# Score blocks trimmed of their masked corner in 64x64 tiles, and another written-out order of the later steps, in a fused window-attention and swish kernel

## The chip, the cores and the metric

The kernel runs on one core of a Trainium2 chip. The core has a matrix engine (PE in the profile, its weight loads PEld), three engines for elementwise work (DVE, ACT, POOL), and DMA queues (those of SP, POOL and ACT are used here). The metric is the device time of one execution in microseconds. Three executions of the kernel before took 222.1, 220.78 and 221.57 us; their median, 221.57 us, is the time before.

## What is computed

Attention with a sink of 4 keys and a window of 128 keys, over 4 batches, 8 heads, 768 positions and 64 features per head; the result goes, as 3072 tokens of 512 features, through a two-layer network with a swish that has a factor beta per hidden feature:

```python
pos = np.arange(S)                                  # S = 768
rel = pos[:, None] - pos[None, :]
keep = (pos[None, :] < n_sink) | ((rel >= 0) & (rel < window))   # n_sink 4, window 128
scores = np.where(keep, q @ k.T / sqrt(64), -1e9)   # per batch and head
attn = softmax(scores) @ v
x = attn as [3072 tokens, 512]
h = x @ w_in                                        # [512, 2048]
g = h * (1 / (1 + exp(-beta * h)))
out = g @ w_out                                     # [2048, 512]
```

A query block of 128 positions therefore needs its own key block (kept where the key does not lie after the query), the key block before it (kept where the key lies less than 128 back, which is the opposite triangle), and the four sink keys.

## The kernel before

**Units and tiles.** Two heads of one half of a batch (384 positions, three blocks of 128) make a unit; there are 32, four to each of eight half batches. Half batches 0, 2, 4, 6 hold key and query blocks 0 to 2 of a batch (called even below), half batches 1, 3, 5, 7 blocks 3 to 5 (odd). Blocks of scores, 128 keys by 128 queries, are of three kinds: `s` (key block 0 with its sinks), `d` (a query block with its own key block, the diagonal) and `p` (a query block with the key block before it: the "next" block, seen from the key). Four blocks of one kind of place make a tile, which lies in two PSUM banks, one for each head, and becomes one buffer `E` after the exponential (L887, ACT, 1024 columns) and two masks (POOL L902, or DVE L896 and L906). `tiles_of` lists the tiles. In the odd half batches from number 3 on, a pair of units has three tiles: `dpdp` for each unit (key blocks 3 and 4, each with two query blocks side by side) and one tile of four lone blocks, `ddpp`: own block 5 of both units and next block 2 to 3 of both. Even half batches have a tile `dddd` of lone own blocks.

**Steps.** Work for the matrix engine is cut into steps, written as letters in the string `later` and executed in its order, except that a planner (`Graph.arrange`) may take one of the next three groups first when it expects the first one to wait. T: transposes of q and k (L726). S: a burst of up to three score tiles (`SC`, and `band` for half batches 2 and up, L825), its exponentials and masks, and in some the sink scores of a half batch (L918). A: the product with v of one unit (L963, L974), or of four units at once for units 20 to 23 and 28 to 31 (L947, L974), and the division by the sum of weights (DVE L978, L980). R: the transposition of the result; from unit 12 on it is a transposing DMA on SP's queue and has no matrix work. H: 128 hidden features for 384 tokens, four matmuls of 384 columns (L1018), the tanh (ACT L1023) and the product (DVE L1025). O: four of the sixteen matmuls of 512 columns of an output block of 128 tokens (L1041); the fourth such step of a block ends with the eviction (ACT L524 or DVE L530) and the store, which is issued from POOL's queue (L1059).

H0 is the first H step, and so on. H(16T+m) makes hidden block m of token group T (384 tokens). O steps from O12 on: O(12T+4t+j) is part j of block t of group T, needs the hidden blocks 4j to 4j+3 of the group, and keeps one PSUM bank from part 0 to part 3. A8 is the unit 8; the letters that take four units at once are called A20 and A28 here. S8 to S20 go through `band`; S11, S12, S15, S16, S19 and S20 are the six bursts of odd half batches, and each holds two tiles `dpdp` and one `ddpp`. S8 holds the two tiles of units 8 and 9, S9 the tile `dddd` of half batch 2 and one tile of units 10 and 11, S10 the last tile of these units.

**Score matmuls of `band`.** The array is used as four sub-arrays of 64 rows by 64 columns: the row half is the head (64 features of contraction), the column half `c` the half of the key block (64 keys). For a key block with both its own and its next query block (`dp`), each half `c` streams 192 of the 256 queries, from 64c on, since the rest is masked for these keys. All other key blocks stream all their columns: 256 for `s`, 128 for a lone `d` or `p`:

```python
a, z_ = (KW * c, 128 + KW * c + KW) if kinds == "dp" else (0, 128 * len(cols))   # KW = 64
```

The four matmuls of a key block (c = 0, 1, and the two heads for each) follow one another, then those of the next key block. In `band` the numbers 3.5 ns and `(z_ - a) / 2.4 + 2` are only the planner's estimates.

**Queues.** Each engine runs its own list in order. The planner deals out casts, masks and evictions among ACT, DVE and POOL, and lays down the order of SP's and POOL's DMA issues, with estimated costs.

Of the kernel before, what the change touches and what calls it, by code (L numbers as in the profile page):

```python
# [395 lines left out]
def _program(nc, G, sb, ps, q, k, v, w_in, w_out, beta, out):  # L396
    NU = 2 * NPAIR
    NSTG, NX, NV, NT, NE, NON, NG, NTT, NOS, NWS = 2, 2, 3, 12, 7, 6, 3, 3, 4, 6
# [4 lines left out]
    NK = NB // 2  # L403
# [17 lines left out]
    qkT = sb("qkT", (128, NT, 2, HALF), BF16)  # L421
# [24 lines left out]
    BAND, KW = 8, 64  # L446
    LANES, QUADS = [6,7], [5,7]
    P = ps("P", (128, 8, 512))

    def add(eng, fn, ns, r=(), w=(), x=(), dma=None, after=(), hold=550, chain=None):  # L450
        return G.add(eng, fn, ns, r, w, x, dma, None, after, hold, chain)
# [237 lines left out]
    def qk_keys(u, name="qkT", every=NT):  # L689
        return [(name, u % every, a, c) for a in range(2) for c in range(NK)]  # L690
# [111 lines left out]

    def band(tiles, bs):

        got, free, now = [], {}, 0.0
        for j, t_ in enumerate(tiles):
            jobs = {}
            for i, (kind, u, kb, qb) in enumerate(TILES[t_]):
                jobs.setdefault((u, kb), []).append((qb, i, kind))
            for (u, kb), cols in sorted(jobs.items(), key=lambda x: x[1][0][1]):  # L810
                half = u // 4 % 2
                own_ = u if kb >= NK * half else u - 4
                kc, q0, i0 = (kb % NK) * 128, (cols[0][0] - NK * half) * 128, cols[0][1]
                kinds = "".join(x[2] for x in cols)
                for c in range(2):
                    a, z_ = (KW * c, 128 + KW * c + KW) if kinds == "dp" else (0, 128 * len(cols))
                    for hh in range(2):
                        rows = slice(64 * hh, 64 * hh + 64)
                        at = max(now, free.get((hh, c), 0.0))
                        if got:  # L820
                            got[-1][3] = at - now
                        now, free[hh, c] = at + 3.5, at + (z_ - a) / 2.4 + 2
                        got.append([lambda e, rows=rows, own_=own_, kc=kc, u=u, q0=q0, a=a, z_=z_, bk=bs[2 * j + hh],
                                    i0=i0, c=c:
                                    e.matmul(P[KW * c:KW * c + KW, bk, 128 * i0 + a:128 * i0 + z_],  # L825
                                             qkT[rows, own_ % NT, 1, kc + KW * c:kc + KW * c + KW],
                                             qkT[rows, u % NT, 0, q0 + a:q0 + z_], start=True, stop=True),
                                    qk_keys(u) + (qk_keys(own_) if own_ != u else []), bs[2 * j + hh], 0.0])
        got[-1][3] = max(free.values()) - now
        for fn, keys, bk, ns in got:  # L830
            add("pe", fn, ns + 3.5, r=keys, x=[("B", bk)])

    def SC(n):
# [18 lines left out]
        if TILES[tiles[0]][0][1] >= BAND:  # L852
            band(tiles, bs)
# [382 lines left out]
    for x in "T0:63 T1:01 S1:01 T2:64 T3:46 S0:12 S4:56 S3:34 S2:01 F:2 V:5 A1:1 A0:5 A2:4 R0:5 A3:2 R1:0 R2:4 R3:0".split():  # L1236
        x, _, bk = x.partition(":")
# [5 lines left out]
        elif x == "F":  # L1243
            G.begin()
            bk = take(1)
# [9 lines left out]
    for x in "".split():  # L1255
        x, _, bk = x.partition(":")
# [20 lines left out]
    for x in early:  # L1277
# [5 lines left out]
        if x[0] == "T":  # L1283
# [3 lines left out]
                OT=4 + sum(x[0] == "R" for x in early), H=sum(x[0] == "H" for x in early), load=24)  # L1287
    n_cast[0], n_w[0] = 20, 8
    last = "O"
    later = ("AAAAHOORORORROHHHHHHHHHHTTOTOOSTOOOOSSOOHHHAAAAHHRHRRORHOOOSOOOOOSAROARHHHHARHARHHHHHHHHHH"  # L1290
             "OOOOOOSOOOOSOOHHHARARARARHHHHHHHHHHHHHOOOOOOSOOOOOSOHHHHHHHHHHHHHHHHARRRROOOOSOOOSOOOOARAR"
             "ARARHHHHHHHHHHHHHHHHHHHHHHHHHOOOSOOOOOSOOOHHHHHARRRRHHOOOOOOOOHHHHHHHHHHHHHHHHOOOOOOOOOOOO"
             "OOOOOOOOOO")
    for c in later:
        s = {"S": "SC", "R": "OT", "A": "AV"}.get(c, c)
        while True:
# [4 lines left out]
            now = G.free["pe"]  # L1301
# [41 lines left out]
```

## Time and profile before

| | us |
|---|---|
| median of three executions | 221.57 (220.78 to 222.10) |
| the profiled execution, its own time | 222.19 |
| its span, first to last instruction | 220.1 |
| lies around the span | 2.1 |

The profiled execution is 0.62 us above the median. The span is divided below into what the matrix engine does and what it waits for; a group's row gives the busy time, the mean length of one instruction in ns (which overlaps its neighbours', because matmuls are pipelined), and the idle time before it with what ended it. The chain of waits gives start, length and the work or wait, with the number of instructions.

### The profile page before, as it was taken

The numbers are of one execution on the slowest core, as the hardware profiler recorded it, in microseconds if no ns is written. First come the engines' busy times: TensorE is split into PE (matmuls) and PEld (weight loads), VectorE is DVE, ScalarE is ACT, GpSimd is POOL, SyncE is SP. The second block draws the span as 40 slices with busy tenths as digits, with TensorE's granted clock in tenths as the row PEclk, the third lists the DMA queues.
The fourth block names the chain that finished last, engine by engine and source line by source line (L and its number), as shares of the span: only waits on it lengthen the run. The fifth ranks groups of instructions, "written<-read, shape, count | busy, mean of one in ns | idle before, by whom it ended". The sixth has DMA issues, their size and how long they took to land.

```text
span 220.1 us, 4804 instructions
## 1 busy us (share of the span) xinstructions
PE 211.7 (96%) x1893; PEld 120.2 (55%) x1915; DVE 136.1 (62%) x297; ACT 148.8 (68%) x245; POOL 69.2 (31%) x132
## 2 busy tenths in 40 slices
PE   8889899999999999999999999999999999999995
PEld 2455457565475466546654566546665456465443
DVE  2687699898786379444980489557885248088000
ACT  2698799586875897459774698195987674187211
POOL 8213552211550682036202761152101770100100
PEclk9999999999999999999999999999999999999999
DMA  6999989999979999599975999879859022400122
GB/s 195 234 292 362 354 212 370 387 316 211 209 168 149 223 172 258 81 220 218 216 120 135 209 209 202 170 167 246 119 98 189 28 81 53 130 2 0 51 95 95
DMA packets 94718, 39.88 MB, mean 181 GB/s; under 512 B 82072, under 2 KB 89512, under 8 KB 94696
## 3 DMA queue, kind: packets, MB, share of 16 engines
q1 hardware_dynamic: 91928, 33.28, 70.6%
q0 software_dynamic: 1680, 5.51, 7.6%
q10 hardware_dynamic: 1088, 0.79, 1.1%
q8 instruction: 15, 0.25, 0.5%
q14 instruction: 7, 0.06, 0.1%
HBM read 27.37 MB, written 6.29 MB: 153 GB/s over the span
## 4 chain that ended last, share of the span: by engine, by line
PE 83%; SPq 7%; DMA 5%; DVE 3%; issue 1%; ACT 0%
PE P L1041 37%; PE P L1018 35%; DMA g<-in_moe_w_in_dram 5%; PE P L974 4%; SPq L605 4%; PE P L825 4%; SPq L617 2%; DVE E L906 1%; PE P L963 1%; SPq L1252 1%; DVE g L1025 1%; PE P L726 1%; DVE w_in L529 1%; PE P L1000 1%; PE P L918 1%
## 5 line engine op out<-in xcount | busy, mean ns | idle before, releaser
L1018 PE MATMUL P<-xT,w_in 128*128 128x384 bf16 x512 | 87.0, 326 | 1.3 <-POOL w_in L526 1.0
L1041 PE MATMUL P<-w_out,g 128*128 128x512 bf16 (+2 forms) x380 | 83.5, 370 | 1.7 <-issue 1.0
L1023 ACT ACTIVATE t<-P,hbeta 128x384 f32<-128x384 f32 x128 | 71.8, 586 | 17.9 <-PE P L1018 13.2
L1025 DVE SCALAR_TENSOR_TENSOR g<-t,P 128x384 bf16<-128x384 f32 x128 | 67.7, 551 | 20.8 <-ACT t L1023 15.9
L1018 PEld LDWEIGHTS P<-xT,w_in 128*128 128x128 bf16 x512 | 49.0, 98 | 34.3 <-POOL w_in L526 1.4
L1041 PEld LDWEIGHTS P<-w_out,g 128*128 128x128 bf16 x400 | 37.3, 98 | 40.4 <-issue 0.5
L887 ACT ACTIVATE E<-P 128x1024 bf16<-128x1024 f32 x44 | 43.2, 1032 | 11.4 <-PE P L825 10.9
L902 POOL TENSOR_SCALAR_AFFINE_SELECT E<-E 128x512 bf16<-128x512 bf16 x57 | 36.8, 670 | 31.8 <-ACT E L887 31.7
L1059 POOL DMA_DIRECT2D out_dram<-osb x21 | 11.9, 568 | 57.9 <-ACT osb L524 57.9
L524 ACT ACTIVATE osb<-P 128x512 f32<-128x512 f32 x13 | 7.8, 598 | 25.5 <-PE P L1041 25.5
L980 DVE TENSOR_TENSOR onorm<-P,rden 128x384 bf16<-128x384 f32 x32 | 17.8, 555 | 0.9
L974 PE MATMUL P<-vaug,E 128*128 128x65 bf16 x352 | 15.1, 193 | 0.0
L530 DVE TENSOR_SCALAR osb<-P 128x512 f32<-128x512 f32 x10 | 6.9, 690 | 13.0 <-PE P L1041 12.9
L974 PEld LDWEIGHTS P<-vaug,E 128*128 128x128 bf16 x352 | 14.1, 97 | 1.3
L529 DVE CAST vaug<-v_stage 128x512 bf16<-128x512 f32 x19 | 9.5, 502 | 8.4 <-DMA v_stage<-in_v_dram 8.3
L896 DVE TENSOR_TENSOR E<-E,maskS 128x512 bf16<-128x512 bf16 x16 | 7.0, 464 | 8.6 <-ACT E L887 8.5
L1261 PE MATMUL P<-const-bfloat16-1.0 128*128 128x512 bf16 (+1 forms) x35 | 11.2, 443 | 1.1 <-PEq L1325 0.8
L524 ACT ACTIVATE k<-k_stage 128x512 bf16<-128x512 f32 (+1 forms) x13 | 7.8, 603 | 2.1 <-DMA k_stage<-in_k_dram 2.0
L825 PEld LDWEIGHTS P<-qkT 64*64 64x64 bf16 x336 | 6.4, 106 | 5.2 <-issue 4.7
L698 POOL TENSOR_TENSOR kS<-qkT,headm 128x8 bf16<-128x8 bf16 (+1 forms) x10 | 2.3, 230 | 22.1 <-DMA qkT<-k 12.7
L825 PE MATMUL P<-qkT 64*64 64x192 bf16 (+2 forms) x336 | 8.7, 239 | 0.0
L526 POOL TENSOR_SCALAR_AFFINE_SELECT q<-q_stage 128x512 bf16<-128x512 f32 x6 | 4.1, 690 | 14.2 <-DMA q_stage<-in_q_dram 14.2
(66 smaller groups left out, 123.2 us busy)
## 6 DMA issues: line engine op xcount, KB each, us to landing
v_stage<-in_v_dram SPq DMA_DIRECT2D x24, 256.0 KB, 4.7
out_dram<-osb POOLq DMA_DIRECT2D x21, 256.0 KB, 3.0
q_stage<-in_q_dram SPq DMA_DIRECT2D x15, 256.0 KB, 5.2
k_stage<-in_k_dram SPq DMA_DIRECT2D x15, 256.0 KB, 5.2
wst<-in_moe_w_in_dram SPq DMA_DIRECT2D x5, 512.0 KB, 8.2
wst<-in_moe_w_out_dram SPq DMA_DIRECT2D x4, 512.0 KB, 7.6
g<-in_moe_w_out_dram SPq DMA_DIRECT2D x4, 512.0 KB, 6.6
q_stage<-in_q_dram SPq DMA_DIRECT2D x2, 768.0 KB, 7.8
```

The source lines that it names most:

```text
L524: return lambda e: e.activation(dst, src, AF.Copy, bias=0.0, scale=scale)
L529: return lambda e: e.tensor_copy(dst, src)
L825: e.matmul(P[KW * c:KW * c + KW, bk, 128 * i0 + a:128 * i0 + z_], qkT[rows, own_ % NT, 1, kc + KW * c:kc + KW * c + KW], qkT[rows, u % NT, ...
L887: add("act", lambda e, src=src, dst_=dst_: e.activation(dst_, src, AF.Exp, bias=0.0, scale=SCALE), act_ns(1024), w=[("E", z)] + [("m", z, ...
L902: alts = {"gp": (lambda e, dd=dd, sg=sg: e.affine_select(dd, dd, [[0, n] for n in dd.shape[1:-1]] + [[sg, 128]], ALU.is_ge, 0.0, base=min( ...
L974: e.matmul(A[:, c0:c0 + D + 1], E[t_ % NE][:, i, hh, :], vaug[vz][:, kb % NK, 2 * hp + hh, :], start=a, stop=o, skip_group_check=True), 31,
L980: add("dve", lambda e: e.tensor_tensor(onorm[on][:, :, :, :].rearrange("p m h d -> p (m h) d"), av[:, :, 0:D], rden[on][:, :].unsqueeze(2) ...
L1018: add("pe", lambda e, c=c: e.matmul(hp, w_in16[:, c, m * 128:(m + 1) * 128], xT[:, c, t0:t0 + HALF], start=(c == 0), stop=(c == 3)), mm_ns ...
L1023: add("act", lambda e: e.activation(tt[ti][:, :], hp, AF.Tanh, bias=0.0, scale=hbeta[:, m:m + 1]), act_ns(HALF) + 93, r=["hbeta"], w=[("t" ...
L1025: add("dve", lambda e: e.scalar_tensor_tensor(gt[T_ % NG][:, m, :], tt[ti][:, :], 1.0, hp, ALU.add, ALU.mult), dve_ns(HALF), r=[("t", ti)] ...
L1041: add("pe", lambda e, m=m: e.matmul(P[:, bk, 0:n], gt[T_ % NG][:, m, t * 128:(t + 1) * 128], w_out16[:, m, cols], start=(m == 0), stop=(m ...
L1059: add(eng, lambda e: e.dma_start(out_t[3 * T_ + t], osb[z][:, :]), 262144 / 300, r=[("osb", z)], dma=f"do{eng}{z}", hold={"sp": 550, "gp": ...
```

## The change

Two things are changed. First, in `band`, a lone own block (`d`) streams for the keys 64 to 127 only the queries 64 to 127, and a lone next block (`p`) streams for the keys 0 to 63 only the queries 0 to 63; the corners left out are masked to zero later in any case, by a select that overwrites them. In tiles of four lone blocks the blocks are issued in the order 0, 2, 1, 3 (own, next, own, next in a `ddpp`), and a `p` issues its long half first. The planner's estimate for a score matmul is half a ns longer. Second, thirteen steps of the string `later` change place; the kinds of steps and their number are the same. Read by their numbers, the moves are these:

| step | before | after |
|---|---|---|
| H28 | ahead of A8 | behind A9 |
| H33 | behind R13 | ahead of O23 |
| O24 | behind H47 | ahead of H45 |
| H51 | behind R19 | ahead of A16 |
| R19 | behind A19 | behind H56 |
| O36 | behind H63 | behind H57 |
| S16 | behind O46 | ahead of O46 |
| O47 | ahead of H64 | behind H67 |
| O52 | behind S17 | ahead of S17 |
| A26 (unit 26) | behind R25 | ahead of R25 |
| O59 | behind H104 | ahead of H104 |
| O69 | ahead of H105 | behind R30 |
| H127 | ahead of O78 | behind O84 |

H28, H33 and so on are counted from H0; an A is named by its unit. All steps before A8 (reached 62 us into the profiled execution) and all behind O84 keep their place, but for what the planner makes of it.

```diff
--- before.py
+++ after.py
@@ -802,30 +802,35 @@
 
     def band(tiles, bs):
 
-        got, free, now = [], {}, 0.0
+        got, free, now, todo = [], {}, 0.0, []
         for j, t_ in enumerate(tiles):
             jobs = {}
             for i, (kind, u, kb, qb) in enumerate(TILES[t_]):
                 jobs.setdefault((u, kb), []).append((qb, i, kind))
-            for (u, kb), cols in sorted(jobs.items(), key=lambda x: x[1][0][1]):
-                half = u // 4 % 2
-                own_ = u if kb >= NK * half else u - 4
-                kc, q0, i0 = (kb % NK) * 128, (cols[0][0] - NK * half) * 128, cols[0][1]
-                kinds = "".join(x[2] for x in cols)
-                for c in range(2):
-                    a, z_ = (KW * c, 128 + KW * c + KW) if kinds == "dp" else (0, 128 * len(cols))
-                    for hh in range(2):
-                        rows = slice(64 * hh, 64 * hh + 64)
-                        at = max(now, free.get((hh, c), 0.0))
-                        if got:
-                            got[-1][3] = at - now
-                        now, free[hh, c] = at + 3.5, at + (z_ - a) / 2.4 + 2
-                        got.append([lambda e, rows=rows, own_=own_, kc=kc, u=u, q0=q0, a=a, z_=z_, bk=bs[2 * j + hh],
-                                    i0=i0, c=c:
-                                    e.matmul(P[KW * c:KW * c + KW, bk, 128 * i0 + a:128 * i0 + z_],
-                                             qkT[rows, own_ % NT, 1, kc + KW * c:kc + KW * c + KW],
-                                             qkT[rows, u % NT, 0, q0 + a:q0 + z_], start=True, stop=True),
-                                    qk_keys(u) + (qk_keys(own_) if own_ != u else []), bs[2 * j + hh], 0.0])
+            mine = []
+            for n, ((u, kb), cols) in enumerate(sorted(jobs.items(), key=lambda x: x[1][0][1])):
+                kind = "".join(x[2] for x in cols)
+                for c in (1, 0) if kind == "p" else (0, 1):
+                    span = {"dp": (KW * c, 128 + KW * c + KW), "d": (KW * c, 128), "p": (0, KW * c + KW)}.get(
+                        kind, (0, 128 * len(cols)))
+                    mine.append((n % 2 if len(jobs) == 4 and kind in "dp" else n, j, u, kb, cols, c, span))
+            todo += sorted(mine, key=lambda x: x[0])
+        for _, j, u, kb, cols, c, (a, z_) in todo:
+            half = u // 4 % 2
+            own_ = u if kb >= NK * half else u - 4
+            kc, q0, i0 = (kb % NK) * 128, (cols[0][0] - NK * half) * 128, cols[0][1]
+            for hh in range(2):
+                rows = slice(64 * hh, 64 * hh + 64)
+                at = max(now, free.get((hh, c), 0.0))
+                if got:
+                    got[-1][3] = at - now
+                now, free[hh, c] = at + 3.5, at + (z_ - a) / 2.4 + 2.5
+                got.append([lambda e, rows=rows, own_=own_, kc=kc, u=u, q0=q0, a=a, z_=z_, bk=bs[2 * j + hh],
+                            i0=i0, c=c:
+                            e.matmul(P[KW * c:KW * c + KW, bk, 128 * i0 + a:128 * i0 + z_],
+                                     qkT[rows, own_ % NT, 1, kc + KW * c:kc + KW * c + KW],
+                                     qkT[rows, u % NT, 0, q0 + a:q0 + z_], start=True, stop=True),
+                            qk_keys(u) + (qk_keys(own_) if own_ != u else []), bs[2 * j + hh], 0.0])
         got[-1][3] = max(free.values()) - now
         for fn, keys, bk, ns in got:
             add("pe", fn, ns + 3.5, r=keys, x=[("B", bk)])
@@ -1287,9 +1292,9 @@
                 OT=4 + sum(x[0] == "R" for x in early), H=sum(x[0] == "H" for x in early), load=24)
     n_cast[0], n_w[0] = 20, 8
     last = "O"
-    later = ("AAAAHOORORORROHHHHHHHHHHTTOTOOSTOOOOSSOOHHHAAAAHHRHRRORHOOOSOOOOOSAROARHHHHARHARHHHHHHHHHH"
-             "OOOOOOSOOOOSOOHHHARARARARHHHHHHHHHHHHHOOOOOOSOOOOOSOHHHHHHHHHHHHHHHHARRRROOOOSOOOSOOOOARAR"
-             "ARARHHHHHHHHHHHHHHHHHHHHHHHHHOOOSOOOOOSOOOHHHHHARRRRHHOOOOOOOOHHHHHHHHHHHHHHHHOOOOOOOOOOOO"
+    later = ("AAAAHOORORORROHHHHHHHHHHTTOTOOSTOOOOSSOOHHAAHAAHHRHRRORHOOOSOOOOOSARHOARHHHARHARHHHHHHHOHH"
+             "HOOOOOSOOOOSOOHHHHARARARAHHHHHRHOHHHHHHOOOOOSOOOOSOHHHHOHHHHHHHHHHHHARRRROOOOOSOOSOOOOARAA"
+             "RRARHHHHHHHHHHHHHHHHHHHHHHHHOHOOSOOOOOSOOHHHHHARRRORHHOOOOOOOOHHHHHHHHHHHHHHHOOOOOOOHOOOOO"
              "OOOOOOOOOO")
     for c in later:
         s = {"S": "SC", "R": "OT", "A": "AV"}.get(c, c)
```

## The prediction

> **What bounds the kernel now.** I read the page's busy times first, then the matrix engine's waits from 32.8 us on, then the chain of waits. 220.1 us of span and 2.1 us around it make the profiled execution's 222.19 us, 0.62 above the median of 221.57. I take differences from the one and add them to the other.
>
> ```profile
> PE 211.7 (96%) x1893; PEld 120.2 (55%) x1915; DVE 136.1 (62%) x297; ACT 148.8 (68%) x245; POOL 69.2 (31%) x132
> ...
> PEclk9999999999999999999999999999999999999999
> ...
> L1041 PE MATMUL P<-w_out,g 128*128 128x512 bf16 (+2 forms) x380 | 83.5, 370 | 1.7 <-issue 1.0
> ...
> L1041 PEld LDWEIGHTS P<-w_out,g 128*128 128x128 bf16 x400 | 37.3, 98 | 40.4 <-issue 0.5
> ```
>
> No other engine comes near PE's 96%, and its granted clock is never under nine tenths. The missing 4% is where a better order would have to earn. The waits of PE over the whole execution:
>
> ```profile
> PE P L1018 <- POOL w_in L526: 1.0, 2, 0.8
> PE P L1041 <- issue: 1.0, 6, 0.2
> ...
> PE P L870 <- DVE qkT L529: 0.8, 1, 0.8
> PE P L1000 <- ACT xT L524: 0.4, 1, 0.4
> ```
>
> Asked from 32.8 us to the last matmul, the same view keeps only the second row, 1.0 us on "issue", in front of O steps. The chain shows what that is:
>
> ```profile
> 105.26 8.45 PE P L1018 x52
> 113.76 5.13 PE P L1041 x23
> 118.89 0.68 PE P L825 x32
> 119.57 0.28 PE P L918 x4
> 119.84 0.16 issue
> 120.00 4.26 PE P L1041 x19
> 124.27 0.68 PE P L825 x32
> 124.95 0.16 issue
> 125.11 0.81 PE P L1041 x3
> ```
>
> O steps have four matmuls each, so x23, x19 and x3 each lack one: the first record behind a wait is missing (380 matmuls against 400 weight loads in L1041). H runs at 8.45/52 = 0.1625 us a matmul. With the missing one, 113.71 (105.26 + 8.45) to 118.89 is 24 matmuls at 0.216 us: no gap between H and O at all. Behind S16, 0.16 + 0.81 = 0.97 us stand for four matmuls, 0.86 us; so about 0.1 us is lost there, at the change from 64x64 sub-arrays to the whole array. After 32.8 us, then, PE waits for nobody; it only pays for changes of array shape. **Moving a step can gain nothing there; it can only uncover something.** Gain must come from fewer or shorter matmuls.
>
> **The tile edit.** The time of a score burst follows its streamed columns. Per sub-array, S14 (two `s` of 256, two `dp` of 192) streams 896 columns, S13 1408 (a `dddd` of 4 x 128 more), an odd burst 4 x 192 + 4 x 128 = 1280 (0.68 us, the rows of S15 and S16 above). S13 and S14:
>
> ```profile
> 95.07 0.73 PE P L825 x32
> ...
> 99.36 0.51 PE P L825 x16
> ```
>
> (0.73 − 0.51)/512 = 0.43 ns and (0.68 − 0.51)/384 = 0.44 ns a column; the rest of the 0.51, some 0.12 us, is the change of shape. In a `ddpp` after the change each sub-array streams 128, 64, 128, 64 columns instead of four times 128: the own block leaves its long half on the lower key half and the next block on the upper, so that in the order own, next, own, next both halves carry 384 columns, not 512. That is 128 x 0.43 = 0.055 us for a burst, and six bursts (S11, S12, S15, S16, S19, S20) give **−0.33 us**. The `dddd` tiles gain nothing: their lower halves still stream four times 128 columns, and the upper halves, now 64, wait for them. Instruction counts stay at 336 in L825; masks and exponentials keep their sizes, and the corner now left unwritten is overwritten by the select.
>
> No row here shows matmuls of two lengths side by side, so bounds: at best −0.33; at worst the two lengths never overlap, each sub-array pair takes (128 + 64) x 4 = 768 columns' time instead of 512, 256 x 0.43 = +0.11 a burst, **+0.66 us** in all. I take −0.33: the rows by shape grow with columns down to the shortest, 32 ns and 30 ns for 64 columns, and halves of `dp` with different columns already run side by side.
>
> ```profile
> L825 PE MATMUL P<-qkT 64*64 64x192 bf16 x144 | 5.2, 247 | 0.0
> ...
> L825 PE MATMUL P<-qkT 64*64 64x128 bf16 x144 | 3.6, 217 | 0.0
> ...
> L825 PE MATMUL P<-qkT 64*64 64x256 bf16 x48 | 2.5, 279 | 0.0
> ```
>
> The Trainium skill speaks against it: "TensorE: Matmul & The Clock Gate", Part 3, "The mechanism", has matmuls start and end strictly in program order. By that rule a 64-column half issued behind a 128-column one could not end before it, a pair would last two long halves, and the term would be 0 instead of −0.33; no run here has two lengths in turn, so nothing shown decides. The same page's LDWEIGHTS section gives columns/1.2 ns, an estimate of 53 ns for 64 columns, which a 64-column matmul would not hide; by that too the term is 0.
>
> **The moves.** The same thirteen steps run elsewhere, so PE's work sums to 0. Changes of shape stay as many: every S still follows an O or stands before one (S16 before O46 instead of O47, S17 behind O52). What remains is cover.
>
> A8 and A9 go ahead of H28. Their last masks, of `dddd`, are the first POOL pair, those of units 10 and 11 the second:
>
> ```profile
> 59.67 1.23 POOL L902 TENSOR_SCALAR_AFFINE_SELECT E<-E 128x512 bf16<-128x512 bf16 x2 [1.34 <-ACT E L887]
> 61.68 1.26 POOL L902 TENSOR_SCALAR_AFFINE_SELECT E<-E 128x512 bf16<-128x512 bf16 x2 [0.77 <-ACT E L887]
> ...
> 60.86 1.95 PE P L1018 x12
> 62.81 0.18 PE P L974 x6
> ...
> 63.53 0.65 PE P L1018 x4
> ```
>
> A8 starts at 62.81 − 0.65 = 62.16 with masks ready at 60.90; A10, behind A8, A9 (0.72) and H28, at 63.53 with masks ready at 62.94. Cover 0.6 us: cost 0; without it at most the 0.65 us that H28 stood for.
>
> O69 behind A28 pulls A28 0.86 us ahead (S20 itself is 0.28 us earlier by then):
>
> ```profile
> 176.38 3.65 POOL L902 TENSOR_SCALAR_AFFINE_SELECT E<-E 128x512 bf16<-128x512 bf16 x6 [0.84 <-ACT E L887]
> ...
> 181.49 0.35 PE L947 MATMUL P<-vS,ES 32*128 32x130 bf16 x12
> ```
>
> It would begin at 180.6; S20's six masks end at 180.03 now. Cover 0.6 us, and more for units 30 and 31, whose masks these are: cost 0, else up to 0.86.
>
> H127 behind O84: O87's last matmul needs its product. From the end of H127's matmuls (202.00) to the end of the last product (203.21) is 1.21 us; O85, O86 and three matmuls of O87 are 11 x 0.216 = 2.4 us. Cost 0.
>
> ```profile
> 191.60 10.40 PE P L1018 x64
> ...
> 200.71 2.50 DVE L1025 SCALAR_TENSOR_TENSOR g<-t,P 128x384 bf16<-128x384 f32 x4
> ```
>
> H51 ahead of A16 gives A16 0.65 us more cover, and H33 the same to A13. O24 and O36 need hidden blocks done by then (H32 to H35; H48 to H51, H51 being moved for it) and hold one of eight banks longer. O47 and O59 carry an eviction on ACT or DVE and a store issued from POOL's queue with them; O47's then fall behind the tanh of H64 to H67 instead of ahead of them, with ACT at 68%, and the masks that the store can delay on POOL are S16's, wanted only by A20 (136.60 in the chain below, S16 at 124.27 above). R19 and the order of R25 and A26 move one transposing DMA on SP's queue each; H64 and H96 need them many microseconds later. O52 ahead of S17 changes nothing: five O steps, O48 to O52, already run between A20 and S17, because the planner had swapped them:
>
> ```profile
> 136.60 1.56 PE P L974 x48
> ...
> 138.21 4.26 PE P L1041 x19
> 142.47 0.73 PE P L825 x32
> ```
>
> Bounds of the moves together: no gain (nothing to gain from), a loss of at most 0.65 + 0.86 = 1.5 us if both thin covers fail. I take 0. What lies before A8 and behind O87 is unchanged. **Sum: −0.33 us**, 222.19 to 221.86 for the profiled execution, 221.57 to 221.24 for the median.
>
> **Rivals.** *No gain in the tiles.* If a short half holds its place until the long one beside it is done, a pair lasts two long halves, a tile four of them as now: 0, 221.57. For it: no row shows two lengths in turn. Against: the halves of `dp`, with different columns, do run side by side. The Trainium skill's "TensorE: Matmul & The Clock Gate" would have it so.
>
> *A mask queued behind a cast: slower.* The changed string moves the planner's clock, and with it which cast POOL gets. POOL takes its list in order and casts wait for loads:
>
> ```profile
> POOL q L526 <- DMA q_stage<-in_q_dram: 14.2, 5, 6.1
> ...
> 102.27 1.23 POOL L902 TENSOR_SCALAR_AFFINE_SELECT E<-E 128x512 bf16<-128x512 bf16 x2 [2.20 <-ACT E L887]
> 103.47 0.66 POOL L526 TENSOR_SCALAR_AFFINE_SELECT q<-q_stage 128x512 bf16<-128x512 f32 x1
> ...
> 103.82 0.18 PE P L974 x6
> ...
> 104.42 0.30 PE P L974 x10
> ```
>
> Here a cast follows directly on the masks of units 18 and 19. With H51 put ahead of A16 the planner sees 0.65 us of room and may set the cast first. The masks end at 103.50, A18 begins at 104.42 and then at 105.07: 1.57 us of cover. A cast of 0.66 with the mean wait 14.2/5 = 2.84 uncovers 0.66 + 2.84 − 1.57 = 1.93 us: 223.2. It decides once the cast's load is more than 0.9 us late. Against: here the load was there in time.
>
> *A luckier start: faster.* Before 32.8 us PE waits 1.0 for w_in, 0.8 for the transposed q and k and 0.4 for xT, 2.2 us. Planned anew, half of it could go with the tile gain: 221.24 − 1.1 = 220.1. Against: no step before A8 moves.
>
> *The tiles serialize*: +0.66, 222.2.
>
> **How the numbers follow.** Forecast 0.57, no gain 0.16, the late mask 0.14, the luckier start 0.08, serialized tiles 0.05. Half a per cent, 1.1 us, is about what a measurement of this kernel can tell from no change: the three runs alone span 1.3 us. Same is 220.46 to 222.68. The forecast, no gain and serialized tiles fall within it but for the scatter of medians, some 0.03 either way; the late mask mostly above, the luckier start mostly below: faster 0.10, same 0.76, slower 0.14. The range runs from 220.4 (the lowest run less the gain) to 222.9 (short of the late mask's 223.2, above the serialized tiles).
>
> **What would show it.** Right: odd bursts of 0.62 to 0.63 us in the chain instead of 0.68, even ones unchanged; PE's waits from 32.8 us on still only "issue"; the first O behind H103 and the last H where they stand, moved by what the bursts saved. Lockstep: odd bursts still 0.68. Serialized: 0.79. Late mask: a PE row in L963 or L974 that waits for POOL. The prediction is wrong if PE before 32.8 us changes, or if any PE wait over 0.5 us appears behind it.

## The result, and the profile after

22 executions of each kernel, taken in turn, gave 221.12 us before (220.14 to 222.94) and 220.42 us after (219.40 to 221.31). The ratio is 0.9957, with a 95% interval from 0.9937 to 0.9976: faster by 0.24 to 0.63%, about 0.95 us. The forecast was 221.2 us and no change that can be told. The time lies in the range, but the interval lies wholly below 1, so it moved. Two later comparisons, told below, both gave 0.9935.

The profiled execution of the changed kernel took 219.65 us, with a span of 217.9. Its page, engine by engine and with the granted clock in tenths:

```profile
PE 210.8 (97%) x1893; PEld 119.6 (55%) x1915; DVE 136.0 (62%) x297; ACT 148.1 (68%) x243; POOL 70.1 (32%) x134
...
PEclk9999999999999999999999999999999999999999
```

PE is busy 0.9 us less with as many instructions; two casts went from ACT to POOL. PE's waits over the whole execution (line waited at, what released it, us in total, times, longest):

```profile
PE P L1046 <- issue: 0.9, 6, 0.2
PE P L1266 <- PEq L1330: 0.8, 1, 0.8
PE P L875 <- DVE qkT L529: 0.8, 1, 0.8
PE P L1023 <- POOL w_in L526: 0.3, 1, 0.3
```

From 31 us on the same view holds only the first of these rows. As before, then, PE waits for nobody once it runs; ahead of that, 0.3 us stands for w_in where 1.0 stood. The diff moves lines down by five, so L830 is the L825 of before, L1046 the L1041, L979 the L974. The chain of waits (start, length, work, matmuls):

```profile
60.29 0.18 PE P L979 x6
...
69.10 0.62 PE P L830 x24
...
74.43 0.62 PE P L830 x24
...
116.91 0.62 PE P L830 x24
...
121.37 0.62 PE P L830 x24
...
178.51 0.28 PE P L952 x12
...
205.22 0.65 PE P L1023 x4
205.87 3.88 PE P L1046 x18
```

All six odd bursts are 0.62 us instead of 0.68 (four are shown), and the steps that the prediction looked at (A8 at 60.29, A28 at 178.51, H127 at 205.22) follow without a gap. The groups of L830 by shape show the trim itself:

```profile
L830 PE MATMUL P<-qkT 64*64 64x192 bf16 x144 | 5.2, 247 | 0.0
L830 PE MATMUL P<-qkT 64*64 64x128 bf16 x72 | 3.3, 218 | 0.0
L830 PE MATMUL P<-qkT 64*64 64x64 bf16 x72 | 2.9, 191 | 0.0
...
L830 PE MATMUL P<-qkT 64*64 64x256 bf16 x48 | 2.5, 279 | 0.0
```

Half of the 144 lone matmuls of 128 columns now have 64. But the span is shorter by 220.1 − 217.9 = 2.2 us, seven times what the trim brings. Where it went is read from S8, the first step that the diff touches, as the chain shows it, before and then after:

```profile
54.52 0.51 PE P L825 x16
```

```profile
52.65 0.51 PE P L830 x16
```

1.9 us of the 2.2 had been won before S8 began, where the engines run the same instructions in the same order. From the start of S8's first matmul to the end of the span it is 165.62 us before and 165.30 after, 0.32 less. For the start, the two profiled executions happened to lie near opposite ends of what these kernels do: further profiles of both follow below.

### The profile page after: what moved, and what is told of

It reads as the page before. It is cut to its first block, busy times and chain, and to the rows that moved or that the text cites. A ratio compares the mean times of both kernels' runs of the same rounds, so it can differ in the third digit from the quotient of the medians.

```text
span 217.9 us, 4804 instructions
## 1 busy us (share of the span) xinstructions
PE 210.8 (97%) x1893; PEld 119.6 (55%) x1915; DVE 136.0 (62%) x297; ACT 148.1 (68%) x243; POOL 70.1 (32%) x134
## 4 chain that ended last, share of the span: by engine, by line
PE 83%; SPq 6%; DMA 4%; DVE 3%; issue 1%; ACT 0%
PE P L1046 38%; PE P L1023 35%; DMA g<-in_moe_w_in_dram 4%; PE P L979 4%; SPq L605 4%; PE P L830 3%; SPq L617 1%; DVE g L1030 1%; DVE E L911 1%; PE P L968 1%; SPq L1257 1%; PE P L726 1%; DVE w_in L529 1%; PE P L923 1%; PE P L1005 1%
## 5 line engine op out<-in xcount | busy, mean ns | idle before, releaser
L1023 PE MATMUL P<-xT,w_in 128*128 128x384 bf16 x512 | 88.2, 326 | 0.6 <-POOL w_in L526 0.3
L1046 PE MATMUL P<-w_out,g 128*128 128x512 bf16 (+2 forms) x380 | 84.5, 370 | 1.7 <-issue 0.9
L1046 PEld LDWEIGHTS P<-w_out,g 128*128 128x128 bf16 x400 | 37.3, 98 | 39.6 <-issue 0.5
L524 ACT ACTIVATE osb<-P 128x512 f32<-128x512 f32 x12 | 7.2, 597 | 22.9 <-PE P L1046 22.9
L979 PE MATMUL P<-vaug,E 128*128 128x65 bf16 x352 | 15.0, 193 | 0.0
L979 PEld LDWEIGHTS P<-vaug,E 128*128 128x128 bf16 x352 | 14.1, 97 | 1.2
L530 DVE TENSOR_SCALAR osb<-P 128x512 f32<-128x512 f32 x11 | 7.5, 686 | 11.2 <-PE P L1046 11.1
L1266 PE MATMUL P<-const-bfloat16-1.0 128*128 128x512 bf16 (+1 forms) x35 | 10.4, 416 | 1.1 <-PEq L1330 0.8
L529 DVE CAST q<-q_stage 128x512 bf16<-128x512 f32 (+1 forms) x13 | 5.9, 451 | 7.9 <-DMA q_stage<-in_q_dram 7.9
L524 ACT ACTIVATE k<-k_stage 128x512 bf16<-128x512 f32 (+1 forms) x12 | 7.2, 601 | 4.4 <-DMA k_stage<-in_k_dram 4.4
L830 PEld LDWEIGHTS P<-qkT 64*64 64x64 bf16 x336 | 6.2, 107 | 5.2 <-issue 4.7
L830 PE MATMUL P<-qkT 64*64 64x192 bf16 (+3 forms) x336 | 8.4, 233 | 0.0
```

Of the source, the lines that this page charges most:

```text
L524: return lambda e: e.activation(dst, src, AF.Copy, bias=0.0, scale=scale)
L529: return lambda e: e.tensor_copy(dst, src)
L979: e.matmul(A[:, c0:c0 + D + 1], E[t_ % NE][:, i, hh, :], vaug[vz][:, kb % NK, 2 * hp + hh, :], start=a, stop=o, skip_group_check=True), 31,
L1023: add("pe", lambda e, c=c: e.matmul(hp, w_in16[:, c, m * 128:(m + 1) * 128], xT[:, c, t0:t0 + HALF], start=(c == 0), stop=(c == 3)), mm_ns ...
L1046: add("pe", lambda e, m=m: e.matmul(P[:, bk, 0:n], gt[T_ % NG][:, m, t * 128:(t + 1) * 128], w_out16[:, m, cols], start=(m == 0), stop=(m ...
```

## The experiments

The letters of theories belong to the text they stand in. Ratios are against the kernel before, timed in turn with it; a run without an interval is one execution, with its profile. "S13 to S15" and the like are the times between the first score matmuls of two bursts.

**The same two kernels again, and each part alone.** The first two runs repeat the kernels before and after as they are. The two others put one part of the diff into the kernel before: the new `band` with the old string `later`, and the old `band` with the new string.

> The kernel before, unchanged, timed against itself: it gives the scatter. Theory A (the start scatters from run to run with the moment at which the matrix engine's clock is granted in full, and all that the change does is the 0.33 us of the tiles): ratio 1.000 within 0.003; in its profile the stretch from H16 to the end is again 176.7 us, odd bursts 0.68 us, while the time up to H16 differs from 43.4 us by up to 1.5 us. Theory B (the start is fixed for a program, and the new one has a better start): the time up to H16 is again 43.4 us within 0.3.

> The changed kernel once more. Theory A: H16 to the end 176.35 us again, the time up to H16 anywhere from 41.5 to 43.5 us; ratio nearer to 0.9985 than to 0.9957. Theory B: the time up to H16 is 41.5 us again within 0.3, ratio 0.9957.

> The new score blocks with the old order of steps. Theory A: H16 to the end 176.3 us (176.67 less 0.33), odd bursts 0.62 us; ratio 0.9985, like that of the whole change when both are timed together. Theory B (the moves bring the rest, some 0.6 us): ratio 0.9985 while the whole change is at 0.9957, so that the two differ by 0.6 us. Lockstep of unequal halves: odd bursts 0.68 us, 176.67.

> The old score blocks with the new order of steps. Theory A: H16 to the end 176.67 us, no wait of the matrix engine behind 36 us, ratio 1.000. Theory B: ratio 0.997 (0.6 us), and the place shows as a shorter start or a stretch of under 176.3 us from H16 to the end. If moves cost cover: over 176.9 us.

| kernel | median, us | ratio and interval | profile's span | S8 to end | S13 to S15 | S17 to S19 |
|---|---|---|---|---|---|---|
| before, again | 221.37 | 1.0001 [0.9979, 1.0022] | 219.2 | 166.21 | 23.83 | 27.08 |
| after, again | 220.12 | 0.9935 [0.9912, 0.9958] | 218.6 | 165.30 | 23.82 | 27.08 |
| tiles alone | 220.69 | 0.9981 [0.9956, 1.0006] | 218.1 | 165.72 | 24.10 | 26.35 |
| order alone | 236.46 | 1.0669 [1.0630, 1.0709] | 235.8 | 181.8 | 32.86 | 34.27 |

The kernel before repeats, and so does the gain. By their ratio the tiles alone bring about a third of it, and no change lies inside their interval. From S8 to the end their profile is not shorter than the 165.62 us of before: the 0.32 us of the tiles are spent again, 0.28 at A18, which waits (told below), and 0.14 between S15 and S19. There the planner, with the new blocks and the old string, issues S17 one O step later than in the row of before (S17 to S19 is 0.73 us less for that), and the first O matmul behind S18's sink scores starts 0.31 us after the first of them instead of 0.17. The same 0.13 to 0.14 us is lost in the other programs in which S17 stands there (the tiles with H51 alone, and the new order with O36 back, both below).

The new order alone costs about 15 us (the median is of five executions; a sixth took 238.84). None of the expectations gave a loss of this size. The order is no improvement in itself, and what it does depends on the blocks it is put together with.

**What in the tile edit shortens a burst.** Three variants of the changed kernel: blocks in their old order but trimmed; in turn, with the short half of a next block first; in turn, but at full length (its score matmuls compute the masked corners again).

```diff
# trim, no turn
-  mine.append((n % 2 if len(jobs) == 4 and kind in "dp" else n, j, u, kb, cols, c, span))
+  mine.append((n, j, u, kb, cols, c, span))
# turn, short half first
-  for c in (1, 0) if kind == "p" else (0, 1):
+  for c in (0, 1):
# turn, no trim
-  span = {"dp": (KW * c, 128 + KW * c + KW), "d": (KW * c, 128), "p": (0, KW * c + KW)}.get(
+  span = {"dp": (KW * c, 128 + KW * c + KW), }.get(
```

> The changed kernel with the lone blocks trimmed, but issued one after the other (own, own, next, next) instead of in turn. If matmuls leave the queue strictly in order and each waits only for its own sub-array: the four blocks take 187 ns of streaming, against 160 in turn and 213 untrimmed, so odd bursts of 0.65 us. If each sub-array has a queue of its own: 0.62 us. If unequal halves wait for each other: 0.68 us.

> The changed kernel with the next block's short half issued ahead of its long one. Strict order with independent sub-arrays: the long half has to wait until the short one has found its sub-array free, 187 to 190 ns, odd bursts of 0.65 us. Queues of their own: 0.62 us as in the changed kernel.

> The changed kernel with its lone blocks issued in turn, but at full length, so that the masked corner is computed again (it is masked to zero later, as in the kernel before). Theory A (the trim brings the gain, the issue in turn nothing): the odd bursts are 0.67 to 0.68 us as in the kernel before. Rival (issuing in turn brings it): 0.62 to 0.64 us. Since the planner then estimates these blocks as long as the old ones, the same reserve of banks is expected to come on as in the new order with the old blocks: time 234 to 238 us by that cause, 220 to 222 us if the banks depend on the order alone and not on the estimate.

One execution each: 222.66, 221.83 and 239.03 us. Two odd bursts in the chain of the variant with the short half first, and the same two at full length:

```profile
70.31 0.62 PE P L830 x24
...
75.64 0.62 PE P L830 x24
```

```profile
70.92 0.68 PE P L830 x32
...
76.30 0.68 PE P L830 x32
```

From the burst's first matmul to the next step's, S11 takes 0.677 us in the kernel before and at full length, and 0.629 in all three trimmed kernels. So the trim brings the 0.048 us, and the order in which the blocks are issued brings nothing. The start times of one `ddpp`, in the variant with the short half first, show why (ns from the burst's first matmul; each row stands for both heads):

```
issued  block  half          columns  starts
1       own    keys 0-63     128      +354
2       own    keys 64-127    64      +361
3       next   keys 0-63      64      +410
4       next   keys 64-127   128      +389
```

The fourth begins before the third. Its sub-array has been free since the short second one; the third still waits behind the first. Each sub-array works down its own list, so a burst is as long as the fullest list, in whatever turn the blocks are issued. Loading the weights doesn't show behind a short matmul either: on its sub-array the next one starts 28 ns after the one of 64 columns (+361 to +389). That the three single executions are slower than the changed kernel, by up to 19 us, has another cause in the main, told with the banks below.

**H51 ahead of A16.** In the tiles-alone profile, S13 to S15 is 0.28 us longer than in the kernel before. This is where the prediction had put its late mask (units 18 and 19, in front of A18), but in the old order, not the new one. To tell whether moving H51 matters there, the step was moved alone (with the new blocks and otherwise the old order), and moved back alone in the changed kernel; the latter, the tiles alone and the changed kernel were then timed once more beside one another.

```diff
# tiles and H51 alone: old string with the new blocks
-  "OOOOOOSOOOOSOOHHHARARARARHHHH...
+  "OOOOOOSOOOOSOOHHHHARARARARHHH...
# H51 back: the changed kernel
-  "HOOOOOSOOOOSOOHHHHARARARAHHHHHRHO...
+  "HOOOOOSOOOOSOOHHHARARARAHHHHHHRHO...
```

> The new score blocks with the old order, in which only H51 goes ahead of A16. In the profile of the new blocks with the old order A18 waited 0.37 us for its masks, because exponentials stood behind a cast of v that waited for its load. Theory A (the order's worth lies in cover where an early start meets the pace of the loads): this wait is gone, H16 to the end comes to 176.4 us give or take waits elsewhere, and the ratio lies between that of the new blocks alone (0.998) and that of the whole change (0.994 to 0.996). Theory B (the other moves bring it): the ratio stays at 0.998. The planner may also answer with a new bank order: then waits of H on DVE appear.

> The changed kernel with H51 put back behind A19. Theory A: A18 waits some 0.3 to 0.4 us again in the profile when the start is early (H16 before 42 us), and the ratio to the kernel before is 0.997 to 0.998, against 0.9935 to 0.9957 with H51 in front. Theory B: no such wait, ratio as that of the whole change.

> The changed kernel once more, timed together with the next two. Four of five profiles gave 165.30 us from S8 to the end, against 165.62 us for the kernel before, and the stretch ahead of S8 scatters from 52.3 to 54.5 us. Theory C (the start is chance, and all that the change does behind it is the 0.32 us of the tiles and the absence of a wait of 0.6 us behind S19): ratio 0.998, and no lower than that of the kernel with H51 put back. Theory D (this program has a better start): ratio 0.994 to 0.996 a third time, 0.4 us under the kernel with H51 put back.

> The changed kernel with H51 back behind A19, again: its stretch from S8 to the end was 165.30 us like that of the changed kernel, its order ahead of S8 is the same. Theory C: the same ratio as the changed kernel within 0.002. Theory D: 0.002 above it again (0.9967 against 0.9935 to 0.9957).

> The new blocks with the old order, again. Theory A and C: from S8 to the end 165.3 us, with 0.3 to 0.4 us more where A18 waits (165.6 in the first profile), ratio 0.998 to 0.9985. Theory D: the same.

| kernel | H51 ahead of A16 | median, us | ratio and interval | S13 to S15 in the profile |
|---|---|---|---|---|
| tiles and H51 alone | yes | 220.72 | 0.9975 [0.9948, 1.0002] | 23.81 |
| H51 back | no | 220.49 | 0.9967 [0.9944, 0.9989] | 23.82 |
| changed, third time | yes | 220.29 | 0.9935 [0.9906, 0.9965] | 23.82 |
| H51 back, second time | no | 221.00 | 0.9985 [0.9952, 1.0017] | 24.20 |
| tiles alone, second time | no | 221.28 | 0.9980 [0.9945, 1.0016] | 24.31 |

The timeline of the tiles alone, second time, around A16 to A19 (start, length, engine and operation, in brackets the idle time before it and what ended it):

```profile
100.12 0.63 ACT L524 ACTIVATE vaug<-v_stage 128x512 bf16<-128x512 f32 x1 [2.80 <-DMA v_stage<-in_v_dram]
100.66 1.00 ACT L892 ACTIVATE E<-P 128x1024 bf16<-128x1024 f32 x1
...
102.81 1.23 POOL L907 TENSOR_SCALAR_AFFINE_SELECT E<-E 128x512 bf16<-128x512 bf16 x2 [0.54 <-ACT E L892]
...
104.10 0.48 PE L979 MATMUL P<-vaug,E 128*128 128x65 bf16 x10 [0.27 <-POOL E L907]
```

A cast of v on ACT waits 2.80 us for its load; the exponentials are queued behind it, the masks on POOL wait for these, and the last four matmuls of A18 (the first four of the x10) for the masks. The same rows of the changed kernel in its first profile:

```profile
98.97 0.63 ACT L524 ACTIVATE vaug<-v_stage 128x512 bf16<-128x512 f32 x1 [2.62 <-DMA v_stage<-in_v_dram]
99.50 1.00 ACT L892 ACTIVATE E<-P 128x1024 bf16<-128x1024 f32 x1
...
101.65 1.23 POOL L907 TENSOR_SCALAR_AFFINE_SELECT E<-E 128x512 bf16<-128x512 bf16 x2 [0.53 <-ACT E L892]
...
102.32 0.34 PE L979 MATMUL P<-vaug,E 128*128 128x65 bf16 x6
...
103.28 0.47 PE L979 MATMUL P<-vaug,E 128*128 128x65 bf16 x10
```

Here too the cast is late, but the masks are done at 102.88 and these matmuls of A18 begin at 103.28, with 0.40 us to spare. Counted from the first matmul of S13, these masks end anywhere from 8.15 to 10.04 us, in kernels of either order, as the loads fall:

| profile | masks of units 18, 19 end | S13 to S15 |
|---|---|---|
| H51 behind A19: before (four), H51 back | 8.50, 9.00, 9.20, 9.41, 9.45 | 23.82 or 23.83 |
| tiles alone | 9.83 | 24.10 |
| H127 alone | 9.89 | 24.16 |
| H51 back, second time | 9.93 | 24.20 |
| tiles alone, second time | 10.04 | 24.31 |
| H51 ahead of A16: changed (five), tiles and H51 alone | 8.15, 8.72, 9.32, 9.33, 9.81, 9.86 | 23.81 to 23.82 |

In the old place the stretch grows by what the masks end after 9.55 us, in all four rows. In the new place masks that end at 9.81 and 9.86 cost nothing, where the old one would have charged 0.26 and 0.31. So H51 ahead of A16 is cover that is used: worth 0.3 to 0.5 us in the executions in which v is late (four of the nine profiles with H51 in its old place), and nothing in the others. (The programs in which the banks run short, below, are left out here.) The medians alone don't part these kernels: where both were timed in one comparison, the mean span is 218.51 us with the changed kernel and 219.04 with H51 back, a difference of 0.53 with an uncertainty of about as much. By the ratios Theory D came true (0.9935 a third time, 0.9985 with H51 back), but not by its reason: of the 0.89 us between the mean times of these two, 0.35 lies around the span (told below), and with H51 back S8 begins at 53.17 and 52.84 us in the two profiles, no later than in the changed kernel (next table).

**H127, and the start.** The kernel before with only H127 behind O84; and two profiles more of each kernel as it is.

```diff
-  "...HHHHHARRRRHHOOOOOOOOHHHHHHHHHHHHHHHHOOOOOOOOOOOO"
+  "...HHHHHARRRRHHOOOOOOOOHHHHHHHHHHHHHHHOOOOOOOHOOOOO"
```

> The kernel before with a single move, H127 behind O84, in the last 20 us. From S8 to the end 165.62 us, as before. Theory C: ratio 1.000 within 0.002. Theory D: a change at the end can shift the start of a program, so that the ratio may stand 0.003 off while the stretch from S8 to the end is unchanged.

> The kernel before, one more profile, to see which waits of the matrix engine come and go from execution to execution. The stretch from H16's first weight load to the end was 176.89 us without a wait and 177.68 us with two (0.26 us at the transposes near 50 us, 0.56 us behind S19). Theory A (the order takes away waits that only an early start meets): with an early start (H16 before 42 us) a wait of 0.3 us or more behind A8, in steps that the change moves or steps next to them. Theory B (the start alone differs, by chance): 176.9 us plus only what is lost ahead of A8.

> The same as the run before it: one more profile of the kernel before, with the same expectations.

> The changed kernel, one more profile. Both theories: waits ahead of A8 as in the kernel before, up to 0.5 us. Theory A: none behind A8, so that from A8 on the stretch is that of the first profile within 0.1 us, whatever the start. Theory B: waits behind A8 as often as in the kernel before.

> The same as the run before it: one more profile of the changed kernel, with the same expectations.

H127 alone gives 221.56 us, ratio 0.9992 [0.9962, 1.0021]: nothing, as costed. The five profiles that each kernel has by now (the run with H127 counted with before, whose start it shares):

| | before | after |
|---|---|---|
| first matmul of S8, us | 54.45, 52.97, 54.00, 52.51, 53.85 | 52.58, 53.31, 53.31, 54.02, 52.48 |
| from there to the end | 165.62, 166.21, 165.61, 165.61, 165.95 | 165.30, 165.30, 165.31, 165.31, 165.30 |

The start scatters over 1.5 to 1.9 us in both; the means, 53.56 and 53.14, do not part. One place at which it scatters is the filler at the very start, matmuls on a constant, before and then after in the first profiles:

```profile
0.85 4.85 PE L1261 MATMUL P<-const-bfloat16-1.0 128*128 128x512 bf16 x11 [0.85 <-PEq L1325]
```

```profile
0.85 4.04 PE L1266 MATMUL P<-const-bfloat16-1.0 128*128 128x512 bf16 x11 [0.85 <-PEq L1330]
```

The same eleven matmuls take 0.81 us longer in one, and what follows starts 0.77 us later (5.50 and 4.73). Others are casts that wait for loads. The filler alone doesn't decide when S8 begins: it takes 4.85 us also in the profile of before with the earliest S8 (52.51), where hardly anything waits afterwards, and 3.90 us in one with a late S8 (54.00). From S8 on, the changed kernel is the same to 0.01 us in five executions, and the kernel before has 0.34 us more in one of five (A18, as above) and 0.60 in another, where an O step behind S19 waits for the exponentials of the sinks on ACT:

```profile
PE P L1041 <- ACT ES L922: 0.4, 1, 0.4
```

The means are 165.80 against 165.30, of which the tiles are 0.32 and these waits 0.18. The second wait came up in this one profile only, of the fifteen of kernels whose banks don't run short; that the new order keeps it away isn't shown.

**Why the new order alone is so slow.** PE's waits with the new order and the old blocks, and three H steps between H58 and H63 in the timeline, with the O steps behind them:

```profile
PE P L1018 <- DVE g L1025: 10.3, 15, 1.3
```

```profile
112.08 0.82 PE L1018 MATMUL P<-xT,w_in 128*128 128x384 bf16 x4 [1.26 <-DVE g L1025]
114.16 1.46 PE L1018 MATMUL P<-xT,w_in 128*128 128x384 bf16 x4 [1.26 <-DVE g L1025]
116.89 1.46 PE L1018 MATMUL P<-xT,w_in 128*128 128x384 bf16 x4 [1.26 <-DVE g L1025]
118.14 3.16 PE L1041 MATMUL P<-w_out,g 128*128 128x512 bf16 x8
```

Each H waits until the product of the H before it has emptied a bank, as if there were one bank only. The waits are not the whole loss. The second and third of these H steps take 1.46 us for four matmuls, where the first takes 0.82; the eight matmuls of 512 columns behind them take 3.16 us, where eight at 99.45 us take 1.90. The page shows the granted clock down in the two slices from 112 to 124 us:

```profile
PEclk9999999999999999999679999999999999999999
```

It was 0.66 from 112 to 118 us and 0.77 from 118 to 124. Of the 9.03 us by which S13 to S15 is longer than in the kernel before, the waits are 5.67 (four of 1.26, one of 0.62), and the slower matmuls some 2.5. The six executions of this kernel go by their mean granted clock, too: 234.9 us at 1.000, 236.08 and 236.46 at 0.993, 237.47 to 238.84 at 0.986.

The waits themselves have a reason in the planner's code:

```python
LANES = [6, 7]; SOON = 2200
reserve[0] = t is not None and t < G.free["pe"] + SOON               # an S step is expected
runs = [[j] for j in (LANES if reserve[0] else range(8)) if j not in held]
```

When it expects a score burst within 2.2 us, it keeps all banks but 6 and 7 for it. Counted while the planner lays out the program, this holds for 27 H steps with the new string and the old blocks, among them H58 to H63, and O36, put ahead of H58, holds bank 6 until its block is done: H58 to H63 all go through bank 7; H87 to H104 have both and wait every other time, mostly for 0.61 us. In the changed kernel it holds for one H step, in the kernel before and with the tiles alone for none. The string was put back at one place, O36 behind H63:

```diff
-  "HOOOOOSOOOOSOOHHHHARARARAHHHHHRHOHHHHHHOOOOOS...
+  "HOOOOOSOOOOSOOHHHHARARARAHHHHHRHHHHHHHOOOOOOS...
```

> The new written-out order with the old lone blocks, but O36 put back behind H63. Theory A (the 15.5 us that the new order lost with the old blocks come from a reserve of banks that an H step opened under it can't use, so that H58 to H63 all go through one bank, and the loss is in the stretches from S13 to S15 and from S17 to S19): with O36 no longer open ahead of H58, those steps alternate between two banks; S13 to S15 is 24 to 27 us instead of 32.9, S17 to S19 is within 1 us of the 27.1 us of the kernel before, and the time is 221 to 226 us. Rival (the moves themselves, O36 not among the costly ones, bring the loss): both stretches stay within 1 us of 32.9 and 34.3 us and the time is 235 to 238 us.

223.44 us, beside 220.71 for the kernel before in the same run, one execution each: some 12 of the 15 us are gone. S13 to S15 is 26.18 instead of 32.86 us, and S17 to S19, 26.35, waits no more (S17 itself stands one O step later). That second stretch isn't freed by a bank: the move shifts the planner's clock, and the reserve, which hangs on it, now holds for 12 H steps only, H87 to H101 not among them. What is left are two H steps and an O step that wait, with two banks in turn:

```profile
110.87 1.47 PE L1018 MATMUL P<-xT,w_in 128*128 128x384 bf16 x8 [0.61 <-DVE g L1025]
112.96 1.47 PE L1018 MATMUL P<-xT,w_in 128*128 128x384 bf16 x8 [0.61 <-DVE g L1025]
115.05 3.19 PE L1041 MATMUL P<-w_out,g 128*128 128x512 bf16 x14 [0.61 <-DVE g L1025]
```

The same reserve is at work in the variants of the tile edit. In the program at full length it again holds for 27 H steps, and S13 to S15 is 31.59 us, S17 to S19 36.05; in the two trimmed variants, for 11, and S13 to S15 is 24.60 in both. The string `later` of the change thus fits its own blocks and their estimates alone: issuing the same matmuls in another turn is enough to bring the reserve on.

**What lies around the span.** Every execution lists its time and its span, and the difference hardly varies within a program:

| program | executions | time less span, us |
|---|---|---|
| before | 84 beside others | 2.04 to 2.18 |
| H127 alone; H51 alone with the tiles; H51 back | 48 | 2.02 to 2.17 |
| tiles alone | 24 | 1.90 to 2.00 |
| trim, no turn; turn, short half first | 2 | 1.93, 1.96 |
| changed kernel, all three times | 43 | 1.68 to 1.81 |
| new order with the old blocks; O36 back; turn, no trim | 8 | 1.71 to 1.80 |

The changed kernel has 0.37 us less around its span than the kernel before. It shares that with the slowest kernels of this study, so it doesn't come with being fast, and putting H51 back takes it away. The profile shows nothing there, and I did not find the cause.

The gain, from the means of the two later comparisons (26 executions of before and 9 of after; 35 and 12):

| | first | second |
|---|---|---|
| time | 221.50 − 220.16 = 1.34 | 221.64 − 220.25 = 1.39 |
| span | 219.40 − 218.43 = 0.97 | 219.52 − 218.51 = 1.01 |
| around the span | 2.10 − 1.73 = 0.37 | 2.12 − 1.74 = 0.38 |

The first comparison has no spans of the kernel before; its mean times differ by 0.95 us, so that 0.37 around the span would leave 0.58 in it. Of these 0.6 to 1.0 us in the span, each with an uncertainty of some 0.4, the tiles are 0.32 and the waits at A18 and behind S19 about 0.2, as far as five profiles tell. The remaining 0.1 to 0.5 us is not settled: it may lie ahead of S8, where the scatter of five profiles hides it, in waits behind S8 that five profiles caught too seldom, or be chance in these means.

## Why the prediction was right and wrong

**The bound and the tiles: right.** PE sets the time, and in the first profile of the changed kernel it waits for no other engine from 31 us on. The odd bursts went to 0.62 us in the chain; per burst the trim brought 0.048 us for the 0.055 worked out, S13 and S17 with their `dddd` another 0.007 each where nothing was expected, and from S8 to the end 0.32 for 0.33. The lockstep and the serialized tiles fell. The rule of the Trainium skill that stood for the first (“TensorE: Matmul & The Clock Gate”, Part 3, “The mechanism”: matmuls start and end strictly in program order) isn't what the trace shows, with a start at +389 ns for a matmul issued after one that starts at +410. The argument for the price was right for a reason other than the one given: the change of turn, to which the prediction tied the balance of the halves, isn't needed.

**“Moving a step can gain nothing there; it can only uncover something”: the step that failed.** It was read from one profiled execution without a wait. Others with H51 in the old place do wait, at A18 by 0.28 to 0.49 us, where a load of v comes late (four profiles of nine), and the kernel before once behind S19 by 0.60; the changed kernel did neither in five profiles. The prediction saw the place and the mechanism, a mask behind a late cast before A18, and gave H51 “0.65 us more cover” at a value of 0. It took the wait for something that the new order might bring. At A18 it was something the old order had now and then and the new one removes: a gain where the rival put a loss of 1.93, and a cast on ACT, not one on POOL, that brings it. The cover was misread as well: 104.42 is where A18's first matmuls are found, but those that need the masks are its last four, at 104.78 in the same chain. With 0.36 us more cover the rival's loss would have come to 1.57.

**“I take differences from the one and add them to the other”: the second failure, and the larger piece that is certain.** The 2.1 us around the span were taken as a constant. They are 1.73 in the changed kernel, a term of −0.37 us that the sum does not have. No row of the profile of before could have told that, and the cause stays open.

**The start.** The luckier start was put at 1.1 us with a chance of 0.08, and the first two profiles look just like it: 1.9 of 2.2 us won ahead of S8. Over five profiles of each kernel the start is mostly chance, and a difference of a few tenths is left open. The prediction would have called itself wrong if PE before 32.8 us changed. That sign says little, since the kernel before changes there from one execution to the next.

**The other moves.** A8 and A28 kept their cover, H127 cost nothing (0.9992 alone), and five O steps stand between A20 and S17 as before. Writing O52 there was not idle, though: with the new blocks and the old string the planner puts six, at a cost of 0.14 us behind S18. The steps with their evictions and stores cost nothing in the changed kernel: S8 to the end is 0.32 us less, just the tiles, with no row of PE's waits against it. But the bound of 1.5 us for a loss was too narrow as reasoning: that O24 and O36 “hold one of eight banks longer” was passed over at no cost, and with the old blocks the place of O36 alone decides some 12 of the 15 us lost. In the changed kernel it is harmless because the planner's reserve, which the prediction did not read, holds for one H step there.

## What to carry to other kernels

One profiled execution without a wait does not prove that a step has cover enough: where the releaser hangs on a load, compare several profiles of the kernel, or ask by how much the load may be late. A hand-written order of steps is right for one set of estimates only; change a block's shape and it has to be found anew, and a step that holds a bank over a row of others must be costed with the banks that are really open to them at that place. And below a per cent, what lies around the span has to be compared too, before a gain is looked for in the schedule.

## What the runs showed of the hardware

The four 64x64 sub-arrays take matmuls independently: one whose sub-array is free starts ahead of one issued before it (+389 against +410 ns), and three issue orders of the same trimmed blocks take 0.629 us each. The time of an execution less its span hardly varies within a program and differs between programs: 1.73, 1.97 or 2.10 us, each within 0.1, for programs of the same work; why is not known. In the new order with the old blocks, waits of 1.26 us ahead of one H step after another went with a granted clock of 0.66 and 0.77 over 12 us, in which eight matmuls of 512 columns took 3.16 us instead of 1.90. It does not follow each time: one of the six executions kept a mean clock of 1.000, and in the variant at full length the clock stayed up through four such waits.
